# Attention with memory and two expert layers on one core: the opening in token pairs, padded queries and a new order

## The chip, the core and the metric

One Trainium2 chip, one of its cores. The engines are TensorE (PE, with its weight loads shown apart as PEld), VectorE (DVE), ScalarE (ACT), GpSimd (POOL) and SyncE (SP), which here issues most transfers. The metric is the device time of one execution in microseconds; the time of a kernel is the median of its runs.

## The reference

Attention over four sequences of 768 tokens, eight heads of 64. The sequence is cut into chunks of 32 queries; each chunk attends to 8 memory slots and to its own keys with 16 to the left and 8 to the right (64 columns in all, fewer at the sequence's ends). The result goes through two layers, 512 to 2048 to 512 each, the first with a leaky ramp, the second with a rational function of `h`.

```python
for c in range(S // 32):
    l_start, r_end = max(0, 32 * c - 16), min(S, 32 * c + 32 + 8)
    k_full = concat([mem_k, k[:, :, l_start:r_end]], axis=2)      # v_full alike
    scores = scale * q_c @ k_full.T                               # scale = 1 / sqrt(64)
    a = exp(scores - max(scores))
    out[:, :, c_start:c_end] = (a / (sum(a) + 1e-09)) @ v_full
x = out.transpose(0, 2, 1, 3).reshape(3072, 512)
h = x @ w_in;  x = maximum(0.01 * h, h) @ w_out
h = x @ w_in2
P = a0 + a1*h + a2*h*h + a3*h*h*h
y = (P / (1 + |b0|*|h| + |b1|*h*h + 1e-6)) @ w_out2
```

## The kernel before

The 3072 tokens go through the layers in six tiles of 512. Weights and activations are split into a high and a low part, so each product of the layers is three matmuls (high x high, high x low, low x high). A weight chunk is 128 of the 2048 hidden columns; there are 16 for each of the four matrices, and each is loaded once, split by `pair_scale` (ACT), `pair_join` (three whole-tile operations on DVE), `pair_hi` (a cast on ACT) and `pair_lo` (a difference). `pair_load(0, ONE_)` loads the first input chunk, `emit_first(i, ...)` runs the first layer's input matmuls of chunk i for the first tile. After the opening, the attention blocks of the later tiles are spread between the chunks' matmuls.

The order of every instruction on every engine is written out by hand (`tc.manual_schedule()`): the order of the calls is the order in each engine's queue. Every queue is in order, so an instruction that waits holds what stands behind it. SP's transfers signal through eight completion slots: an issue waits until the transfer eight issues earlier has landed.

The opening, up to the first chunks of the first layer, makes the first tile's attention: 512 tokens in U = 4 units of 128 tokens. Its functions, for unit u:

- `unit_k`, `unit_q`: four 128 x 128 transposes (`turn`, L414) of the loaded keys or queries into PSUM; keys copied by ACT into `okT` (two tiles, one for each half of the heads, early[4] and early[5]), queries scaled by ACT into `oqT`. Loads are by 128 tokens in rows of 64 floats (256 bytes) per head.
- `unit_small`: the transposed memory keys and the keys at unit borders, copied by DVE (L424, L428).
- `unit_b`: copies on GpSimd that put each key chunk also into the ring of left neighbours (L445).
- `unit_s`: scores, 32 matmuls (L464), each with one head's 32 queries as 64 x 32 weights on 64 columns; the trace has two records for each.
- `unit_m` (L472 to L476), on DVE: a mask for the first unit, the maximum, the difference. `unit_e` (L480): exp on ACT.
- `unit_n` (L486 to L489): DVE sums, adds 1e-9 (the "guard", a tiny `tensor_scalar`, L487) and takes the reciprocal (L488); then a product, on GpSimd for units 0 to 2, on DVE for unit 3.
- `unit_t` (L495 to L502): four transposes of the probabilities, copied out by ACT into `pT` (zero-padded, in two half copies, for units 0 and 1; one plain copy for 2 and 3).
- `unit_x`: values, matmuls with `vroom[u]` as weights (L514 for units 0 and 1, 16 matmuls; L527 for units 2 and 3, 32 matmuls). `vroom` holds the value rows of each window, with the 8 memory rows copied there by `room_mem` on GpSimd (four copies on 8 partitions, L418, 2048 or 1536 columns).
- `side_h`, `side_l`: attention output from PSUM into `xh` (ACT, L538) and the remainder into `xl` (DVE, L542), the first layer's input.

`heat(n)` is n matmuls of 128 columns on the identity (L966) and `warm(n)` one of n x 128 columns (L969); nobody reads their results. The last output tile is written 128 tokens at a time: 3 matmuls a chunk into one PSUM bank (L950), a copy (L955), a transfer of 256 KB (L956).

## Time and profile before

| what | value |
|---|---|
| median of 3 runs | 1138.33 us (1136.58 to 1138.68) |
| profiled execution: time, span | 1139.2 us, 1137.4 us |
| busy: PE, PEld | 1128.2 us (99%), 923.3 us (81%) |
| busy: DVE, ACT, POOL | 766.3 us (67%), 628.9 us (55%), 238.3 us (21%) |
| PE busy 0 to 32.60 us | 27.93 us |
| chain that ended last | 96% PE, 1% DVE, 1% DMA |

The profile is of one execution; its own time stands 0.9 us above the median. TensorE is busy nearly throughout, so the chain that ended last is almost all TensorE; the rest of it lies in the first 33 us. Times in the profile are counted from the span's start.

### The profile page before, as it was taken

To read this page: it belongs to the slowest core of one execution; us is meant where nothing else is said; L and a number is where in the kernel's file an instruction comes from. 1 tells how busy PE (TensorE), PEld (TensorE's weight loads), DVE (VectorE), ACT (ScalarE), POOL (GpSimd) and SP (SyncE) were. 2 spreads that over 40 slices of the span, in tenths; PEclk is the share of its full clock that TensorE was granted. 3 is DMA by queue.
4 is the path that set the end of the run, shared out by engine and by line. 5 is a ranking of instruction groups with operands and counts; after the bars stand their busy time and mean duration, and the time that the engine had idled before them with its cause. 6 is when DMAs were issued, how large, how long until landed. Compare 5 with 4: busy or idle time off the path is not lost.

```text
span 1137.4 us, 19661 instructions
## 1 busy us (share of the span) xinstructions
PE 1128.2 (99%) x7626; PEld 923.3 (81%) x7626; DVE 766.3 (67%) x1315; ACT 628.9 (55%) x1138; POOL 238.3 (21%) x274
## 2 busy tenths in 40 slices
PE   8999999999999999999999999999999999999998
PEld 6777788888888888888888888888888888888887
DVE  5988754555645555542346886887887887788775
ACT  5687522232232223223347777776776777777765
POOL 5000302132211332210000222221222222222222
PEclk9999999999999999999999999999999999999999
DMA  9967777787778778732343002001001100100001
GB/s 193 277 200 214 181 218 208 210 244 216 207 212 232 198 206 236 214 114 94 93 140 117 22 1 74 1 1 61 14 1 40 36 1 19 57 1 4 35 0 37
DMA packets 146921, 131.59 MB, mean 116 GB/s; under 512 B 61744, under 2 KB 117392, under 8 KB 146828
## 3 DMA queue, kind: packets, MB, share of 16 engines
q1 hardware_dynamic: 141604, 122.80, 37.8%
q0 software_dynamic: 4864, 7.45, 2.9%
q8 instruction: 60, 0.98, 0.4%
q14 instruction: 33, 0.27, 0.1%
q10 hardware_dynamic: 360, 0.08, 0.0%
HBM read 92.52 MB, written 37.75 MB: 115 GB/s over the span
## 4 chain that ended last, share of the span: by engine, by line
PE 96%; DVE 1%; DMA 1%; ACT 0%; issue 0%; SPq 0%; POOL 0%; DVEq 0%; POOLq 0%
PE hps L854 45%; PE acc L950 23%; PE acc L912 23%; PE psx L754 2%; PE pss L712 1%; PE pss L554 0%; DMA early<-in_q_dram 0%; PE psx L601 0%; DMA pb<-park_dram 0%; PE pss L464 0%; PE psk L377 0%; PE hps L842 0%; DMA park_dram<-pb 0%; PE psq L414 0%; PE psx L527 0%
## 5 line engine op out<-in xcount | busy, mean ns | idle before, releaser
L912 PE MATMUL acc<-g,w 128*128 128x512 f32 x1152 | 278.3, 391 | 0.0
L950 PE MATMUL acc<-w,g 128*128 128x512 f32 x1152 | 275.4, 389 | 0.0
L950 PEld LDWEIGHTS acc<-w,g 128*128 128x128 f32 x1152 | 216.3, 188 | 44.8
L912 PEld LDWEIGHTS acc<-g,w 128*128 128x128 f32 x1152 | 214.8, 188 | 45.1
L890 POOL TENSOR_TENSOR g<-R,g 128x512 fp32r<-128x512 f32 x96 | 124.7, 1299 | 503.9 <-ACT g L889 465.7
L864 ACT ACTIVATE g<-hps 128x512 fp32r<-128x512 f32 x96 | 57.4, 598 | 299.2 <-PE hps L854 299.2
L854 PE MATMUL hps<-xh,w 128*128 128x512 f32 x752 | 205.0, 395 | 0.0
L854 PE MATMUL hps<-yh,w 128*128 128x512 f32 x768 | 204.1, 389 | 0.0
L867 DVE TENSOR_TENSOR g<-s,g 128x512 fp32r<-128x512 f32 x96 | 66.2, 690 | 175.9 <-ACT s L865 172.8
L854 PEld LDWEIGHTS hps<-yh,w 128*128 128x128 f32 x768 | 144.2, 188 | 30.0
L854 PEld LDWEIGHTS hps<-xh,w 128*128 128x128 f32 x752 | 138.4, 188 | 29.5 <-DVE w L195 0.2
L677 POOL DMA_DIRECT2D vb<-in_v_dram x128 | 83.8, 656 | 260.2 <-PE psx L754 201.7
L877 ACT ACTIVATE A<-hps 128x512 f32<-128x512 f32 x96 | 57.2, 596 | 113.9 <-PE hps L854 113.9
L893 DVE SCALAR_TENSOR_TENSOR A<-A,small,pb 128x512 f32<-128x512 f32 x96 | 72.1, 751 | 56.5 <-ACT pb L878 56.4
L854 PE MATMUL hps<-yl,w 128*128 128x512 f32 x384 | 102.6, 389 | 0.0
L854 PE MATMUL hps<-xl,w 128*128 128x512 f32 x376 | 100.9, 390 | 0.0
L884 DVE SCALAR_TENSOR_TENSOR A<-A,pb 128x512 f32<-128x512 f32 x96 | 66.4, 692 | 30.2 <-ACT pb L897 30.2
L854 PEld LDWEIGHTS hps<-yl,w 128*128 128x128 f32 x384 | 72.1, 188 | 14.9
L854 PEld LDWEIGHTS hps<-xl,w 128*128 128x128 f32 x376 | 70.6, 188 | 15.4
L879 ACT ACTIVATE R<-hps,small 128x512 f32<-128x512 f32 x96 | 75.0, 782 | 0.0
L886 DVE SCALAR_TENSOR_TENSOR R<-R,small,A 128x512 f32<-128x512 f32 x96 | 72.2, 752 | 3.4
L895 DVE SCALAR_TENSOR_TENSOR R<-R,small,hps 128x512 f32<-128x512 f32 x96 | 71.8, 748 | 3.4
(126 smaller groups left out, 1140.7 us busy)
## 6 DMA issues: line engine op xcount, KB each, us to landing
wr<-in_moe_w_in_dram SPq DMA_DIRECT2D x32, 512.0 KB
wr<-in_moe_w_out_dram SPq DMA_DIRECT2D x32, 512.0 KB
park_dram<-pb SPq DMA_DIRECT2D x16, 512.0 KB
pb<-park_dram SPq DMA_DIRECT2D x64, 128.0 KB
...
```

The lines of the kernel that those rows point to most:

```text
L677: nc.gpsimd.dma_start(out=vw[r + at:r + at + n, c], in_=v[bi, hs, lo:lo + n, :].rearrange("h p d -> p h d"))
L854: nc.tensor.matmul(ps[:, :n], w_[:, ws], x_[:, kk, :], start=(kk == 0 and m == 0), stop=(kk == KC - 1 and m == 2))
L864: nc.scalar.activation(out=gh, in_=ps, func=AF.Prelu, alpha=0.01)
L867: return [lambda: nc.vector.tensor_tensor(out=gl, in0=s, in1=gh.bitcast(F32), op=ALU.subtract)]
L879: nc.scalar.activation(out=R, in_=ps, func=AF.Identity, scale=ncf[:, 3:4], bias=ncf[:, 2:3])
L884: nc.vector.scalar_tensor_tensor(out=A0, in0=A0, scalar=ONE, in1=U0, op0=ALU.add, op1=ALU.mult)
L886: nc.vector.scalar_tensor_tensor(out=R0, in0=R0, scalar=ncf[:, 0:1], in1=A0, op0=ALU.add, op1=ALU.mult)
L890: nc.gpsimd.tensor_tensor(out=gl, in0=R0, in1=gh.bitcast(F32), op=ALU.subtract)
L893: nc.vector.scalar_tensor_tensor(out=A, in0=A, scalar=babs[:, 1:2], in1=U, op0=ALU.mult, op1=ALU.add)
L895: nc.vector.scalar_tensor_tensor(out=R, in0=R, scalar=ncf[:, 1:2], in1=ps, op0=ALU.add, op1=ALU.mult)
L912: nc.tensor.matmul(acc[i][d][:, :n], w_[:, ws], g_, start=(f == 0 and m == 0), stop=(f == FC - 1 and m == 2))
L950: nc.tensor.matmul(acc[i][s], g_[:, ss], w_, start=(f == 0 and m == 0), stop=(f == FC - 1 and m == 2))
```

## The change

Six parts. (1) The first 256 tokens' keys and queries are loaded as token pairs (two consecutive tokens of one head side by side, rows of 512 bytes), in halves of the heads, and turned four pairs of columns at a time; even and odd tokens are then picked apart by copies of 64 partitions x 256 columns, on ACT for the keys and on DVE for the queries. (2) All queries stand in zero-padded form in `oqB` (early[6] and the new early[7]; both are filled with zeros first, on DVE and GpSimd), so that one matmul takes two heads: 16 matmuls a unit. (3) The warm-up is four 512-column matmuls on a zeroed tile. (4) Order: units 0 and 1 are scored together by halves of the heads, their `unit_m` follow one another, the two `room_mem` copies of the first half move behind the ring copies of unit 2, those of the second half become two transfers in SP's queue, and unit 3's product goes to GpSimd. (5) `pT` of units 2 and 3 is zero-padded too (two fills of 128 x 1024 on GpSimd, two half copies each on ACT), and their values take 16 matmuls; the last unit's second half of values is loaded in four transfers instead of two and its result lies in two banks, copied out by ACT and DVE. (6) The last 128 tokens' output matmuls, copy and transfer are done in two halves of 256 columns.

```diff
-    oqT = early[6].rearrange("p (c m) -> p c m", c=NP)
+    oqB = [t.rearrange("p (c n e m) -> p c n e m", c=NP, e=2, m=CHUNK) for t in early[6:8]]
...
+    def pairs_of(src, g, hs):
+        return src[0, hs, g * 2 * P:(g + 1) * 2 * P, :].rearrange("h (p t) d -> p h (t d)", t=2)
+
+    def load_pairs(raws, src, g, hs=slice(0, H)):
+        nc.sync.dma_start(out=raws[:, hs], in_=pairs_of(src, g, hs))
+
+    def turn_pairs(t, half, ps):
+        for i in range(H // 2):
+            nc.tensor.transpose(ps[:, i * P:(i + 1) * P], t[:, half * (H // 2) + i], ident)
+
+    def pairs_out(ps, o, to, lo, eng, op):
+        for e in range(2):
+            for t in range(2):
+                i = ps[t * 64:t * 64 + 64].rearrange("p (c e m) -> p c e m", c=HP, e=2)[:, :, e, lo:]
+                op(eng, o[e * 64:e * 64 + 64, :, to + 2 * lo + t:to + 2 * P:2], i)
...
             nc.vector.tensor_copy(out=okB[half][:, :, 0:RING, 0:NM],
-                                  in_=i[:, :, 0:NM].unsqueeze(2).to_broadcast([P, HP, RING, NM]))
...
+    def pairs_k(half, eng):
+        ps = psw.tile([P, 512], F32, tag="ps", name="psk")
+        turn_pairs(kpair, half, ps)
+        pairs_out(ps, okT[half], TAT, 0, eng, copy_on)
...
+    def pairs_q(half, eng):
+        ps = psw.tile([P, 512], F32, tag="ps", name="psq")
+        turn_pairs(qpair, half, ps)
+        for e in range(2):
+            for t in range(2):
+                i = ps[t * 64:t * 64 + 64].rearrange("p (c e n m) -> p c e n m", c=HP, e=2, m=CHUNK // 2)[:, :, e]
+                scale_on(eng, oqB[0][e * 64:e * 64 + 64, half * HP:(half + 1) * HP, :, e, t:CHUNK:2], i)
...
-        nc.scalar.mul(out=oqT[:, :, u * P:(u + 1) * P], in_=pv, mul=scale)
+        n, at = P // CHUNK, (u - 2) * P // CHUNK
+        for e, eng in enumerate(engs):
+            r = slice(e * 64, e * 64 + 64)
+            scale_on(eng, oqB[1][r, :, at:at + n, e, :], pv[r].rearrange("p c (n m) -> p c n m", m=CHUNK))
...
         for b in range(2):
...
-                        nc.tensor.matmul(ps[o:o + CHUNK, p, b, :], oqT[r, p, x:x + CHUNK],
-                                         okB[p // HP][r, p % HP, lo:hi + 1:hi - lo, :], start=True, stop=True)
-        ops[u] = ps
+            for p in range(halves[0] * HP, (halves[-1] + 1) * HP):
+                for c in range(2):
+                    n = (2 * u + b) * 2 + c
+                    lo, hi = n % RING, RING + 1 + n
+                    nc.tensor.matmul(ps[c * 64:c * 64 + 64, p, b, :],
+                                     oqB[u // 2][:, p, n % (NQ // 2)].rearrange("p e m -> p (e m)"),
+                                     okB[p // HP][:, p % HP, lo:hi + 1:hi - lo, :], start=True, stop=True)
...
-        if u >= 2:
-            return [lambda: nc.scalar.copy(out=pT[u], in_=ps)]
         return [lambda: part_of(0), lambda: part_of(1)]
...
+        if u not in oxv:
+            if u == U - 1:
+                oxv[u] = [psw.tile([P, 512], F32, tag="ps", name="psx")[:, :256] for _ in range(2)]
+            else:
+                t = (psw.tile([P, 512], F32, tag="ps", name="psx") if u >= 2 else
+                     psa.tile([P, 512], F32, tag="acc", name="psx"))
+                oxv[u] = [t[:, h * 256:(h + 1) * 256] for h in range(2)]
+                oxv[u, "all"] = t
+        xv = [t.rearrange("p (c b h m) -> p c b h m", c=HP, b=2, h=2) for t in oxv[u]]
...
+        for c in cs:
+            for p in ps:
+                for e in range(2):
+                    nc.tensor.matmul(xv[p // HP][e * 64:e * 64 + 64, p % HP, :, c, :], vroom[u][:, c, 2 * p + e, :],
+                                     pT[u][:, (2 * p + c) * 2 + e], start=True, stop=True)
...
+    def side_h(i, ps=ALL, eng=nc.scalar):
+        xv, xh, xl = side(i, ps)
+        copy_on(eng, xh, xv)
...
+            parts = (slice(0, DM // 2), slice(DM // 2, DM)) if (c, s) == (len(items) - 1, ns - 1) else (slice(0, DM),)
+            for ds in parts:
+                for m, (g_, w_) in enumerate(((gh, wh), (gh, wl), (gl, wh))):
+                    nc.tensor.matmul(acc[i][s][:, ds], g_[:, ss], w_[:, ds],
+                                     start=(f == 0 and m == 0),
+                                     stop=(f == FC - 1 and m == 2 and ds.stop == DM))
...
+                parts = (slice(0, DM // 2), slice(DM // 2, DM)) if (c, s) == (len(items) - 1, ns - 1) else (slice(0, DM),)
+                for ds in parts:
+                    nc.scalar.copy(out=e[:, ds], in_=acc[i][s][:, ds])
+                    nc.sync.dma_start(out=out[s0 + s * P:s0 + (s + 1) * P, ds], in_=e[:, ds])
...
+        cold = mall[:, 1].rearrange("p n m -> p (n m)")[:, :P]
+        nc.vector.memset(cold, 0.0)
...
-        nc.sync.dma_start(out=rows_of(kraw[0]), in_=tokens(k, 0, P))
+        nc.vector.memset(early[6], 0.0)
+        nc.gpsimd.memset(early[7], 0.0)
+        LOWER, UPPER = slice(0, H // 2), slice(H // 2, H)
+        load_pairs(kpair, k, 0, LOWER)
...
-        for t, src, u in ((qraw, q, 0), (kraw, k, 1), (qraw, q, 1), (kraw, k, 2), (qraw, q, 2), (kraw, k, 3),
-                          (qraw, q, 3)):
+        load_pairs(qpair, q, 0, LOWER)
+        load_pairs(kpair, k, 0, UPPER)
+        load_pairs(qpair, q, 0, UPPER)
+        for t, src, u in ((kraw, k, 2), (qraw, q, 2), (kraw, k, 3), (qraw, q, 3)):
             nc.sync.dma_start(out=rows_of(t[u]), in_=tokens(src, u * P, P))
...
+                hs = (slice(0, H // 2), slice(H // 2, H)) if (u, c) == (U - 1, 1) else (slice(0, H),)
+                for h in hs:
+                    for b_ in range(2):
+                        load_span(vroom[u][:, c, h], b_ * SB + NM, v, 0, u * P + b_ * QB + c * CHUNK - LCTX, W, h)
...
+                for b_ in range(2):
+                    o, i = mem_rows(1, b_)
+                    nc.sync.dma_start(out=o, in_=i)
...
-        heat(6)
-        unit_k(0, (act, act))
-        unit_q(0)
-        border = unit_small()
-        unit_b(0, pool)
+        for _ in range(4):
+            warm(4, cold)
+        pairs_k(0, act)
+        unit_b(0, pool, (0,))
+        unit_b(1, pool, (0,))
+        unit_small()
+        pairs_q(0, dve)
+        pairs_k(1, act)
+        unit_b(0, pool, (1,))
+        unit_b(1, pool, (1,))
+        unit_s(0, (0,))
+        unit_s(1, (0,))
+        pairs_q(1, dve)
+        unit_s(0, (1,))
+        unit_s(1, (1,))
+        pool.memset(pT[2], 0.0)
+        unit_k(2, (act, act))
+        unit_q(2, (act, act))
+        unit_m(0)
+        unit_m(1)
+        unit_e(0)
+        unit_b(2, pool)
+        pool.memset(pT[3], 0.0)
         room_mem(0, 0, pool)
-        room_mem(0, 1, pool)
-        heat(2)
-        unit_s(0)
-        unit_k(1, (act, act))
-        unit_b(1, pool)
-        unit_q(1)
-        unit_m(0)
-        border()
-        unit_e(0)
-        unit_k(2, (act, act))
-        unit_b(2, pool)
-        unit_q(2)
...
-        room_mem(1, 1, pool)
+        unit_b(3, pool)
+        unit_n(0, pool)
+        unit_q(3, (act, act))
         spread = unit_t(0)
         unit_s(3)
+        room_mem(0, 1, pool)
+        unit_n(1, pool)
...
+        unit_n(3, pool)
+        side_h(0)
+        pair_scale(0, ONE_)
+        run(pair_join(0, ONE_))
...
-        unit_n(3, dve)
-        run(pair_join(0, ONE_))
+        spread = unit_t(3)
+        unit_x(1)
+        unit_x(2)
+        run(spread)
...
-        unit_x(3)
+        side_l(0)
+        side_l(1)
         pair_hi(0, ONE_)
         pair_lo(0, ONE_, pool)
...
         side_h(2)
-        side_h(3)
+        unit_x(3, (0,))
+        unit_x(3, (1,), range(HP))
+        side_h(3, FORE)
+        unit_x(3, (1,), range(HP, NP))
+        side_h(3, REAR, dve)
+        side_l(2)
         emit_first(0, (0, 2))
```

The order at the places that the prediction speaks of follows. TensorE's queue at the program's start, in the kernel before: `hot` is the warm-up, `psk` and `psq` are the turned keys and queries, `pso` the memory keys and borders, `pss` the scores.

```order
L966 MATMUL hot<-ident 128x128 x6
L414 MATMUL psk<-ident,early 128x128 x4
L414 MATMUL psq<-ident,early 128x128 x4
L414 MATMUL pso<-ident,kb 128x24 x4
L966 MATMUL hot<-ident 128x128 x2
L464 MATMUL pss<-early 32x64 x32
L414 MATMUL psk<-ident,early 128x128 x4
L414 MATMUL psq<-ident,early 128x128 x4
L414 MATMUL psk<-ident,early 128x128 x4
L414 MATMUL psq<-ident,early 128x128 x4
L414 MATMUL psk<-ident,early 128x128 x4
L464 MATMUL pss<-early 32x64 x32
```

The same in the changed kernel:

```order
L994 MATMUL hot<-pm 128x512 x4
L425 MATMUL psk<-ident,early 128x128 x4
L414 MATMUL pso<-ident,kb 128x24 x4
L425 MATMUL psq<-ident,early 128x128 x4
L425 MATMUL psk<-ident,early 128x128 x4
L497 MATMUL pss<-early 64x64 x16
L425 MATMUL psq<-ident,early 128x128 x4
L497 MATMUL pss<-early 64x64 x16
L414 MATMUL psk<-ident,early 128x128 x4
L414 MATMUL psq<-ident,early 128x128 x4
L414 MATMUL psk<-ident,early 128x128 x4
L497 MATMUL pss<-early 64x64 x16
```

All four warm-up matmuls stand ahead of the first keys; the scores of the first two units stand together, in halves, behind both halves of the pairs.

DVE's queue at the program's start before, from the copies of the memory keys on (`pss` scores, `pm` probabilities, `mx` and `sm` maximum and sum):

```order
L424 COPY early<-pso 128x2x8x8 x2
L428 COPY early<-pso 128x2x8 x2
L472 MEMSET pss 32x4x16 x2
L475 TENSOR_REDUCE mx<-pss 128x8
L476 TENSOR_TENSOR pm<-pss,mx 128x512
L428 COPY early<-pso 128x2x8 x2
L486 TENSOR_REDUCE sm<-pm 128x8
L487 TENSOR_SCALAR sm<-sm 128x8
L488 RECIPROCAL sm<-sm 128x8
L475 TENSOR_REDUCE mx<-pss 128x8
L476 TENSOR_TENSOR pm_104<-pss,mx 128x512
L475 TENSOR_REDUCE mx<-pss 128x8
```

The same piece of the changed kernel:

```order
L439 COPY early<-pso 128x2x8x8 x2
L443 COPY early<-pso 128x2x2x8 x2
L455 TENSOR_SCALAR early<-psq 64x16x16 x8
L504 MEMSET pss 64x4x16
L507 TENSOR_REDUCE mx<-pss 128x8
L508 TENSOR_TENSOR pm<-pss,mx 128x512
L507 TENSOR_REDUCE mx<-pss 128x8
L508 TENSOR_TENSOR pm_104<-pss,mx 128x512
L518 TENSOR_REDUCE sm<-pm 128x8
L519 TENSOR_SCALAR sm<-sm 128x8
L520 RECIPROCAL sm<-sm 128x8
L518 TENSOR_REDUCE sm<-pm_104 128x8
```

Eight scalings of the queries now stand between the memory keys and the first mask, and both first units' maxima and differences ahead of the first sum.

GpSimd's queue in the kernel before, from the fill of `pT` of unit 0 to the two products behind the second room copies:

```order
L1001 MEMSET pb 128x1024
L1002 MEMSET pb_106 128x1024
L445 COPY early<-early 128x2x4x24 x2
L418 COPY early<-early 8x2048 x2
L445 COPY early<-early 128x2x4x24 x4
L489 TENSOR_TENSOR pm<-pm,sm 128x512
L445 COPY early<-early 128x2x4x24 x2
L418 COPY early<-early 8x1536 x2
L489 TENSOR_TENSOR pm_104<-pm_104,sm 128x512 x2
```

And in the changed kernel (the COPY of 8x2048 are the room copies, those of 128x2x4x24 the ring copies):

```order
L1007 MEMSET early 128x2048
L1037 MEMSET pb 128x1024
L1038 MEMSET pb_106 128x1024
L476 COPY early<-early 128x2x4x24 x4
L1075 MEMSET early 128x1024
L476 COPY early<-early 128x2x4x24 x2
L1082 MEMSET early 128x1024
L434 COPY early<-early 8x2048
L476 COPY early<-early 128x2x4x24 x2
L521 TENSOR_TENSOR pm<-pm,sm 128x512
L434 COPY early<-early 8x2048
L521 TENSOR_TENSOR pm_104<-pm_104,sm 128x512 x2
```

The room copies moved from ahead of nearly everything to between the ring copies and the products; three fills were added.

## Rows read from the trace of the kernel before

**Rows 1.** Busy time by stretch: bounds, length, each engine's busy us, clock, DMA share, GB/s.
```profile
32.60:116.90 84.30, 84.30 (x721) 66.76 (x721) 72.98 (x117) 63.39 (x169) 2.63 (x4) 1.00 0.77 216
116.90:1133.90 1017.00, 1015.97 (x6374) 834.68 (x6372) 673.66 (x1154) 547.88 (x938) 219.45 (x244) 1.00 0.36 104
1133.90:1137.40 3.50, 0.00 (x0) 0.00 (x0) 0.00 (x0) 0.54 (x1) 0.00 (x0) 0.99 0.62 231
```

**Rows 2.** Chain that ended last, up to 60 us: start, length, engine, tile, line.
```profile
21.73 1.05 POOL pm L489
...
22.83 0.66 PE pst L495 x4
...
26.45 0.81 issue
27.25 0.92 PE psx L527 x40
...
28.20 0.59 ACT xh L538
...
32.60 3.12 PE hps L842 x12
```

**Rows 3.** Timeline, TensorE: start, length, operation xcount [idle before and its releaser].
```profile
1.37 2.93 PE L966 MATMUL hot<-ident 128*128 128x128 f32 x12 [1.37 <-POOL ident masks.py:199]
...
4.16 1.12 PE L414 MATMUL psk<-ident,early 128*128 128x128 f32 x4
...
8.69 1.93 PE L464 MATMUL pss<-early 64*32 64x64 f32 x64
...
12.59 0.66 PE L414 MATMUL psk<-ident,early 128*128 128x128 f32 x4
...
13.17 1.10 PE L464 MATMUL pss<-early 64*32 64x64 f32 x64
...
21.03 1.02 PE L969 MATMUL hot<-ident 128*128 128x512 f32 x2
...
23.42 1.15 PE L514 MATMUL psx<-pb,early 128*64 128x64 f32 x32
```

**Rows 4.** Groups by line and shape, first 33 us: busy us, mean ns of one.
```profile
L476 DVE TENSOR_TENSOR pm<-pss,mx 128x512 f32<-128x512 f32 x4 | 2.8, 691 | 0.1
...
L499 ACT COPY pb<-pst 64x512 f32<-64x512 f32 x4 | 2.3, 580 | 0.2
...
L502 ACT COPY pmore<-pst 128x512 f32<-128x512 f32 x2 | 1.2, 588 | 0.4 <-PE pst L495 0.4
...
L1001 POOL MEMSET pb<- 128x1024 f32 x1 | 1.0, 952 | 0.0
...
L488 DVE RECIPROCAL sm<-sm 128x8 f32<-128x8 f32 x4 | 0.8, 203 | 0.1
```

**Rows 5.** Timeline, copies out of PSUM on ACT and DVE.
```profile
5.32 0.65 ACT L418 COPY early<-psk 128x256 f32<-128x256 f32 x2 [3.29 <-PE psk L414]
...
7.64 0.49 DVE L424 COPY early<-pso 128x128 f32<-128x128 f32 x2 [6.12 <-PE pso L414]
...
8.05 0.25 DVE L428 COPY early<-pso 128x16 f32<-128x16 f32 x2
```

**Rows 6.** Timeline, the room copies on GpSimd and what DVE does at the time.
```profile
6.35 3.83 POOL L418 COPY early<-early 8x2048 f32<-8x2048 f32 x2
...
10.73 0.31 DVE L472 MEMSET pss<- 32x64 f32 x2 [2.43 <-PE pss L464]
...
17.54 1.46 POOL L418 COPY early<-early 8x1536 f32<-8x1536 f32 x1
...
17.99 1.04 DVE L487 TENSOR_SCALAR sm<-sm 128x8 f32<-128x8 f32 x1
...
21.18 0.17 DVE L487 TENSOR_SCALAR sm<-sm 128x8 f32<-128x8 f32 x1
```

**Rows 7.** DMA view, first 30 us in 40 slices: GB/s of each.
```profile
GB/s 0 0 60 221 265 228 214 189 215 231 215 222 223 217 217 197 191 168 156 62 160 202 231 133 293 308 150 177 162 156 196 182 197 152 216 299 287 355 382 411
```

151 lines of the change are left out of this document (51 added, 100 removed).

## Prediction

> **What bounds the kernel now.** I read the busy time by stage first. From 32.60 us, where the second weight chunk's first matmul starts, TensorE is busy 84.30 of 84.30 us, and then 1015.97 of 1017.00 us up to 1133.9 [rows 1]. What stands behind 32.60 is therefore a fixed block of 1133.9 - 32.6 = 1101.3 us of TensorE work, and 3.5 us of output behind it. Apart from the last output tile, the diff touches only what lies ahead of 32.60. So the question is when the matmul now at 32.60 starts (call it E); a shift of E is carried whole to the end.
>
> Next I read the chain of waits backwards from E [rows 2]. E follows by 3.8 us the end of the last copy of attention output (28.20 + 0.59 = 28.79). Ahead of that copy stand the last unit's value matmuls at 27.25, after 0.81 us without any compute releaser: the last value rows had not landed. Ahead of that stand the transposes of the softmax, and GpSimd's normalising product at 21.73. So in the old opening two things end within a microsecond of one another: the softmax chain (DVE and GpSimd) and the last value load. A change has to shorten both to gain, and needs to lengthen only one to lose.
>
> **The change part by part.**
> *Warm-up.* Six 128-column matmuls on the identity took 2.93 us, 0.49 each [rows 3]. Now four 512-column ones run on a zeroed tile. That tile is DVE's first instruction, so they can start at about 1.1 instead of 1.37. [...] Four, each 0.05 shorter for running back to back, end at 5.0 if all ran at the high level and at 8.7 if all at the low one. In the old kernel the transposes at 4.16 take 1.12 and the scores at 8.69 take 1.93, against 0.66 and 1.10 at 12.59 and 13.17 [rows 3]: the rise came after 8.69. I take 7.5, nearer the low end. The old keys were transposed at 4.16, so the warm-up now stands ahead of them in TensorE's queue: the opening starts 3.3 us later. What it pays: all that follows runs at the high level. [...]
>
> *Keys as pairs.* Four transposes, 0.66: 7.5 to 8.2. ACT then makes four copies of 64 partitions x 256 columns. A copy of 64 x 512 takes 580 ns and one of 128 x 512 588 ns [rows 4]: half the partitions save nothing. So each costs as much as the old 128 x 256 copy, 0.65 / 2 = 0.33 [rows 5], and four cost 1.3: to 9.55. For two units ACT spends 8 x 0.33 = 2.6 instead of 4 x 0.33 = 1.3.
>
> *Memory keys and borders.* DVE's four copies now wait for ACT's four (they write the same tiles). Two memory copies took 0.49 and two border copies 0.25 [rows 5]: 10.3.
>
> *Queries as pairs.* They go from ACT (two 128 x 512) to DVE: eight of 64 x 256. A DVE copy of 128 columns took 0.49 / 2 = 0.245 [rows 5], an operation of 512 columns 0.69 [rows 4]; 256 columns lie between, 0.37. Four per half: 1.5, to 11.8. These 3.0 us in all are new work on DVE, the engine that makes the softmax, and now stand ahead of it.
>
> *Scores.* 64 matmul records of 32 matmuls took 1.10 at the high level, 0.034 a matmul. The padded form has 16 a unit with weights twice as wide and twice as deep, so 16 cost between 0.55 (same price each) and 1.1 (twice); I take 0.85. Lower half for both units: to 12.7. Then the upper queries' transposes 0.66 (13.4), DVE's next four 1.5 (14.9), and eight matmuls of the first unit 0.45: its scores are complete at 15.4. DVE began its softmax at 10.73 in the old kernel [rows 6]. So the softmax starts 4.7 us later.
>
> *What is given back.* Both first units come together, so DVE need not wait in between (it had idled up to 2.4 us, in the row at 10.73, and some more later). Its list from 15.4: mask 0.15, then for each of four units 2 x 0.69 for maximum and difference and 0.69 + 0.17 + 0.20 for sum, guard and reciprocal. The last product goes from DVE (0.69) to GpSimd (1.05 by the row at 21.73). The units 0 and 1 differences end at 18.3.
>
> *GpSimd's part.* Its order is now: ring copies of unit 2, a zero fill, one memory-room copy, ring copies of unit 3, product 0, the second room copy, products 1, 2, two small copies, product 3. The room copies of 8 x 2048 took 3.83 for two, 1.9 each [rows 6], at 6.35, beside nothing that mattered; now they stand in front of product 0 and product 1. Unit 2's keys are out at 17.1 (scores to 15.8, transposes 0.66, copies 0.65), so: ring 17.75, fill of 0.95 [rows 4] 18.7, room 20.6, ring 21.25. DVE's guard of unit 0 (ready at 19.0) is of the form that took 1.04 instead of 0.17 us while GpSimd was in a room copy, and ended with it [rows 6]; so it ends at 20.8, the reciprocal at 21.0. Product 0: 21.25 to 22.3. Room: 24.2. Product 1: 25.25. On DVE unit 1's sum ends at 21.7, its guard is held to 22.5, reciprocal 22.7, units 2 and 3 maximum and difference to 25.45, unit 2's sum to reciprocal 26.55. Product 2 to 27.6; unit 3's guard is held by it, reciprocal 28.0; product 3 to 29.1. Transposes 0.66: 29.8. Two half copies on ACT, 2 x 0.58 (one copy of 0.59 in the old kernel): 30.95. Last values 1.15, as the sixteen matmuls of the same form at 23.42 [rows 3]: 32.1. Their copy-out is halved over two banks and two engines, 0.35: 32.45. Then the same 3.8 as before: E = 36.25. The same adding, done on the old order, ends 0.3 too late, so 35.95: **3.4 us later than 32.60**.
>
> *The loads.* In SP's queue 29 transfers instead of 25 stand ahead of the third weights, with no more bytes from memory. The last values landed at about 27.2 [rows 2]; here they are wanted at 30.95, so this load is off the path by 3 us either way and I cost it at nothing. If that cover were gone, it would cost up to four issues. [...]
>
> *The tail.* The last tile's matmuls, copy and transfer are halved. In the 3.5 us after the last matmul the output queue still moves 231 GB/s x 3.5 us = 0.81 MB [rows 1], three of the four 256 KB transfers. The last one stands behind this stream, so a copy that ends 0.3 us sooner finds it busy; three more matmul issues cost some 0.1. I take 0 (bounds 0.2 less and 0.1 more).
>
> The profiled execution took 1139.2 us; 3.4 more are 1142.6. The median is 0.9 below the profiled time, so about 1141.7 us.
>
> **The rivals.**
> *B, DVE alone sets the pace.* If GpSimd's instructions fit into gaps and hold nothing, DVE ends its list at 18.3 + 4 x 1.06 + 4 x 0.69 = 25.3, product 3 at 26.4, transposes 27.1, copies 28.3, values 29.4, copy 29.8, E = 33.6, less 0.3: +0.7, so 1139.0. For it: DVE's lists are free of GpSimd except for the guards. Against it: the held guard at 17.99. It decides when the room copies start before 16, which the ring copies ahead of them do not allow, or when they do not hold the guard.
> *C, faster.* If the warm-up runs at the high level early (ends near 5.0, 2.5 sooner) and a 256-column operation on DVE costs what one of 128 does (1.0 sooner), the softmax starts at 11.9, and with B's list E is 29.8, if the last values have landed by 24.8. In the old opening 256-byte runs moved at 189 to 231 GB/s in most slices, the later, longer ones at 287 to 411 [rows 7]. If half of the first 2 MB, 1.05 MB, move at 300 instead of 215, that saves 4.9 - 3.5 = 1.4: they land at 25.85 instead of 27.25, half of their matmuls (0.58), the copy (0.35) and the 3.8 follow, and E is 30.6. So E is 2.0 to 2.8 us sooner; with 2.4, the time is 1135.9. Against it: every old row until 8.69 is at the low level. [...]
> *D, slower still.* If the clock rises only after the warm-up (all four at the low level, 8.7, and three sets of transposes at 1.12), the softmax starts 1.2 + 3 x 0.46 = 2.6 later: +6.0 at most, some of it taken by GpSimd's waits; about 1143.7.
> *The change doing nothing* is not among them: TensorE has no idle time in which a later opening could hide.
>
> **How the numbers follow.** A measurement of this kernel can tell about 0.2%, 2.3 us. Forecast 0.46; D 0.10; B, with what lies between it and the forecast, 0.31; C 0.13. The forecast's own lower end (less than 2.3 later) is counted with B. So slower 0.56, within 0.2% 0.31, faster 0.13. The range leaves out the far part of C and of D: 1136.4 to 1143.9. It is wide since the clock (5.0 to 8.7) and GpSimd's holds (0.7 to 3.4) are not shown by any old row in the new places.
>
> **What would show it.** In the new trace: warm-up rows ending at 6.5 to 8.7, and transposes behind them at 0.66; four ACT copies of 64 x 256 at about 0.33 each; DVE's mask near 15.4 (near 12 would mean C); a guard of about 1 us beside GpSimd's room copy; GpSimd's last product ending near 29; the second chunk's first matmul near 36 (33.5: B; 30: C); TensorE dense behind it. The forecast is wrong if that matmul comes before 35, or if TensorE later shows idle time that the old one hasn't.

## The result and the profile after

The changed kernel takes 1146.48 us (median of 7 runs, 1145.45 to 1147.12) against 1138.68 for the kernel before, measured beside it (7 runs, 1136.58 to 1143.14): 7.8 us slower by the medians; the ratio of the means is 1.0063, 95% interval 1.0044 to 1.0081. Forecast was slower by 3.4 us, 1141.7, with a range to 1143.9. The direction was right and the size less than half; the time lies above the range.

Call E, as the prediction does, the start of the second weight chunk's first matmul. By stretch, the profile after (bounds, length, each engine's busy us, granted clock, DMA share, GB/s):

```profile
0.00:40.46 40.46, 28.80 (x333) 20.64 (x333) 24.96 (x54) 19.80 (x39) 18.07 (x28) 0.92 1.04 249
40.46:1141.48 1101.02, 1099.85 (x7095) 901.67 (x7095) 747.32 (x1270) 610.65 (x1105) 221.44 (x248) 1.00 0.39 110
1141.48:1145.30 3.82, 0.00 (x1) 0.00 (x0) 0.00 (x0) 0.65 (x2) 0.00 (x0) 1.00 0.61 218
```

In the chain of waits E is this row:

```profile
40.46 3.10 PE hps L866 x12
```

E moved from 32.60 [rows 2] to 40.46, by 7.86 us. From E to the end of the last matmul there are 1101.0 us, against 1101.3 [rows 1], and 3.8 behind it against 3.5. So all of the loss is made in the opening and carried whole to the end, as the prediction has it; the question is only what is in those 7.86.

TensorE's opening in the timeline after (start, length, operation, xcount, idle time before it and its releaser), which answers to [rows 3]:

```profile
1.06 5.75 PE L994 MATMUL hot<-pm 128*128 128x512 f32 x8 [1.06 <-DVE early L1004]
...
6.65 0.60 PE L425 MATMUL psk<-ident,early 128*128 128x128 f32 x4
...
7.53 0.66 PE L425 MATMUL psq<-ident,early 128*128 128x128 f32 x4
...
11.36 1.43 PE L497 MATMUL pss<-early 128*64 128x64 f32 x32 [2.74 <-DVE early L455]
...
12.72 1.12 PE L425 MATMUL psq<-ident,early 128*128 128x128 f32 x4
...
15.75 1.97 PE L497 MATMUL pss<-early 128*64 128x64 f32 x32 [1.91 <-DVE early L455]
...
17.66 1.12 PE L414 MATMUL psk<-ident,early 128*128 128x128 f32 x4
...
33.21 1.15 PE L550 MATMUL psx<-pb,early 128*64 128x64 f32 x32
...
34.20 2.04 PE L550 MATMUL psx<-early 128*64 128x64 f32 x64
```

The warm-up ends, and the keys' transposes start, at 6.65. The transposes of the lower queries then run at the high level (0.66 at 7.53), TensorE waits 2.74 us for DVE's query scalings, and what follows is slow again: 1.12 for the upper queries' four transposes, 1.97 for the upper scores, 1.12 for unit 2's keys. The granted clock says the same (same view as the first):

```profile
12.50:15.00 2.50, 1.34 (x10) 0.82 (x6) 1.10 (x3) 0.00 (x0) 0.11 (x1) 0.50 1.14 186
...
17.50:20.00 2.50, 2.29 (x17) 1.89 (x14) 2.27 (x4) 1.14 (x3) 0.66 (x3) 0.72 1.06 201
```

It is at 0.50, the low level, from 12.5 to 17.5, and back between 17.5 and 20 (0.72 on the mean). In the old opening the level was low up to 8.69, rose once and stayed [rows 3]. That is read from durations: in both profiles the granted clock stands at 1.00 throughout the first 10 us, beside rows that took longer than later ones of their form (here 5.75 for the four warm-up matmuls, and 1.02 for one like them at 27.89; before, 1.12 and 0.66 for the keys' transposes), so for the program's start it does not tell the level.

The three other engines around the softmax, from the timeline after; this answers to [rows 6]:

```profile
16.95 0.11 DVE L504 MEMSET pss<- 64x64 f32 x1 [1.35 <-PE pss L497]
...
18.86 0.62 ACT L434 COPY early<-psk 128x240 f32<-128x240 f32 x2 [7.84 <-PE psk L414]
...
19.42 1.19 ACT L453 ACTIVATE early<-psq 64x512 f32<-64x512 f32 x2
...
20.64 0.63 ACT L512 ACTIVATE pm<-pm 128x512 f32<-128x512 f32 x1
...
20.81 1.88 POOL L434 COPY early<-early 8x2048 f32<-8x2048 f32 x1
...
21.30 0.69 DVE L518 TENSOR_REDUCE sm<-pm 128x8 f32<-128x512 f32 x1 [1.46 <-ACT pm L512]
...
22.02 0.70 DVE L519 TENSOR_SCALAR sm<-sm 128x8 f32<-128x8 f32 x1
...
23.24 1.03 POOL L521 TENSOR_TENSOR pm<-pm,sm 128x512 f32<-128x512 f32 x1
...
28.14 1.17 ACT L531 COPY pb<-pst 64x512 f32<-64x512 f32 x2 [1.25 <-PE pst L527]
...
29.34 0.63 ACT L512 ACTIVATE pm<-pm 128x512 f32<-128x512 f32 x1
29.70 0.35 POOL L1105 COPY kT<-early 128x32 f32<-128x32 f32 x2
...
30.08 0.69 DVE L518 TENSOR_REDUCE sm<-pm 128x8 f32<-128x512 f32 x1 [1.51 <-POOL kT L1105]
```

The mask starts at 16.95 (10.73 before). Unit 0's exponential (L512) runs at 20.64, although its input is there at 18.5: ACT's queue has unit 2's key and query copies (18.86 and 19.42) ahead of it. So DVE stands idle for 1.46 us before the sum (L518) at 21.30. Product 0 starts at 23.24. The guard (L519) at 22.02 takes 0.70 beside the room copy at 20.81, and 0.17 at 28.16, where GpSimd stands idle. Unit 3's exponential at 29.34 stands behind the two copies of `pT` of unit 1 (28.14), and DVE is idle again, for 1.5 us, until 30.08. The profile puts that down to GpSimd's small copy, which ends at 30.05, only 0.08 after the exponential; experiment e2 below tells them apart.

The new narrow copies in the groups by shape (busy us, mean ns of one), beside [rows 4, 5]:

```profile
L455 DVE TENSOR_SCALAR early<-psq 64x256 f32<-64x256 f32 x8 | 3.4, 421 | 2.7 <-PE psq L425 2.7
L434 ACT COPY early<-psk 64x256 f32<-64x256 f32 x8 | 3.1, 382 | 5.9 <-PE psk L425 5.3 <-DVE early L443 0.6
```

In these two profiles the loss has two parts. The mask came 6.2 us later (16.95 against 10.73), and from the mask to E it took 23.5 us instead of 21.9, 1.6 more. The forecast had 4.7 for the first and a gain of 1.0 for the second (15.4 to 36.25 is 20.85). The split is that of two single executions: in e8 below, the same old opening had its mask at 8.62 and E at 31.88, which would make it 8.3 and 0.3.

### The profile page after: what moved, and what is told of

Read it like the earlier page. It is cut to its first block, busy times and chain, and to the rows that moved or that the text cites. A ratio compares the mean times of both kernels' runs of the same rounds, so it can differ in the third digit from the quotient of the medians.

```text
span 1145.3 us, 19306 instructions
## 1 busy us (share of the span) xinstructions
PE 1128.7 (99%) x7427; PEld 922.3 (81%) x7427; DVE 772.3 (67%) x1323; ACT 631.1 (55%) x1145; POOL 239.5 (21%) x276
## 4 chain that ended last, share of the span: by engine, by line
PE 95%; DVE 1%; SPq 1%; DMA 1%; ACT 1%; issue 0%; POOL 0%; ACTq 0%; DVEq 0%; POOLq 0%
PE hps L878 45%; PE acc L976 23%; PE acc L936 22%; PE psx L778 2%; PE pss L736 1%; SPq L319 1%; PE hot L994 1%; PE pss L578 0%; DMA pb<-park_dram 0%; PE psx L625 0%; POOL pm L521 0%; PE psk L376 0%; DMA park_dram<-pb 0%; PE hps L866 0%; PE psx L550 0%
## 5 line engine op out<-in xcount | busy, mean ns | idle before, releaser
L878 PEld LDWEIGHTS hps<-xh,w 128*128 128x128 f32 x752 | 138.4, 188 | 29.1 <-DVE w L194 0.2
```

Of the source, the lines that this page charges most:

```text
L878: nc.tensor.matmul(ps[:, :n], w_[:, ws], x_[:, kk, :], start=(kk == 0 and m == 0), stop=(kk == KC - 1 and m == 2))
```

## The experiments

All change the changed kernel, unless it is said otherwise, and compute the whole of it. The table has the three numbers that the argument needs: the start of the first mask on DVE, E, and the time (median of 4 to 12 runs where it says timed, else one execution). The median of the kernel before was 1138.3 beside e9 to e12 (16 runs, 1137.03 to 1140.95) and 1139.1 beside e13 and e14 (23 runs, 1137.37 to 1144.93).

| kernel | mask | E | time |
|---|---|---|---|
| before | 10.73 | 32.60 | 1138.7, timed |
| changed | 16.95 | 40.46 | 1146.5, timed |
| e1 room copies early | 16.98 | 38.75 | 1144.4 |
| e2 exponential 3 first | 16.61 | 38.54 | 1144.4 |
| e3 / e11 clock kept | 16.72 / 15.80 | 39.36 / 38.52 | 1145.0 / 1144.0, timed |
| e4 no token pairs | 13.83 | 37.26 | 1143.3 |
| e5 exponential 0 first | 16.96 | 41.33 | 1147.8 |
| e6 no pairs, order mended | 13.35 | 34.25 | 1141.4 |
| e7 / e10 two warm-ups | 13.41 / 15.62 | 36.06 / 39.12 | 1141.4 / 1143.1, timed |
| e8 old kernel, tail in halves | 8.62 | 31.88 | 1138.3 |
| e9 rebuilt | 9.23 | 32.35 | 1138.5, timed |
| e12 old kernel, new warm-up | 11.03 | 38.54 | 1142.0, timed |
| e13 rebuilt, fewer transfers | 9.56 | 32.47 | 1139.2, timed |
| e14 pairs kept, order mended | 15.33 | 36.36 | 1143.6, timed |

An E of one execution is good to about 0.7 us at best, and a mask to about 2: e8 has the old opening unchanged, and its E is 31.88 instead of 32.60, its mask 8.62 instead of 10.73. Where a row has two runs, they are two executions of one kernel.

**e1, room copies early.**

```diff
+        room_mem(0, 0, pool)
+        room_mem(0, 1, pool)
         pool.memset(pT[2], 0.0)
...
         pool.memset(pT[3], 0.0)
-        room_mem(0, 0, pool)
...
-        room_mem(0, 1, pool)
         unit_n(1, pool)
```

> The changed kernel with its two room copies on GpSimd moved ahead of the first zero fill of pT, into the stretch where GpSimd stands idle (12.6 to 19.3 us in the changed kernel's trace); nothing else. E is the start of the second chunk's first matmul, 40.46 us in the changed kernel. Theory 1 (several queues hold one another: room copies in GpSimd's queue, exponentials behind copies in ACT's queue, the clock's fall): product 1 no longer waits for a room copy and ends about 1.9 us sooner, and E comes 2.0 us sooner, 38.5. Theory 2 (DVE's new query scalings alone set the time): the room copies hold nothing that matters, E stays within 0.3 of 40.5.

Product 1 starts at 24.26 instead of 26.30 (it was to end 1.9 sooner), and E is 38.75, 1.7 us sooner, with the mask where it was (16.98):

```profile
24.26 1.04 POOL L521 TENSOR_TENSOR pm<-pm,sm 128x512 f32<-128x512 f32 x1 [0.41 <-DVE sm L520]
```

Theory 1 holds here: the room copies in front of the products cost 1.7 us at E.

**e2, the exponential of unit 3 first.**

```diff
         unit_x(0)
-        run(spread)
         unit_e(3)
+        run(spread)
```

> The changed kernel with the exponential of unit 3 put ahead of the two copies of pT of unit 1 in ACT's queue; nothing else. Theory 1: the exponential runs at 27.5 instead of 29.3, DVE's 1.5 us of idle time ahead of unit 3's sum falls to nothing, product 3 ends about 1.3 us sooner, and of that 0.9 reaches E (39.6), since the copies and value matmuls of units 1 and 2 then stand in front of unit 3's. Theory 2: DVE's work is in the way, E within 0.3 of 40.5.

```profile
25.41 1.04 POOL L521 TENSOR_TENSOR pm<-pm,sm 128x512 f32<-128x512 f32 x1
...
27.59 0.65 DVE L518 TENSOR_REDUCE sm<-pm 128x8 f32<-128x512 f32 x1
...
29.27 1.04 POOL L521 TENSOR_TENSOR pm<-pm,sm 128x512 f32<-128x512 f32 x1
```

Unit 3's sum now follows without a gap (27.59), so it was the exponential that DVE had waited for, not GpSimd's small copy. From product 1's start to product 3's start it was 31.36 - 26.30 = 5.06 us, and now 29.27 - 25.41 = 3.86: 1.2 us less, as theory 1 expected (1.3). E came 1.9 sooner, more than the 0.9 expected; 0.9 of that is there before product 1 already (25.41 against 26.30), where the edit changes nothing. In this execution the upper queries' transposes and scores ran at the high level (0.66 at 13.27, 1.15 at 15.84). So about 1.0 is the edit's own.

**e3 and e11, the clock kept.**

```diff
+        for _ in range(3):
+            warm(4)
         unit_s(0, (0,))
         unit_s(1, (0,))
         pairs_q(1, dve)
+        for _ in range(2):
+            warm(4)
```

> The changed kernel with three 512-column warm-up matmuls on the identity behind the pairs' first three sets of transposes (TensorE stood idle there from 8.63 to 11.36) and two more behind the upper queries' transposes; nothing else. Theory 1: the granted clock stays at the high level, the upper queries' transposes take 0.66 instead of 1.12, the upper scores about 1.1 instead of 1.97, the mask starts 1.1 to 1.3 us sooner (15.7), and E comes about 1.2 sooner, 39.2. Theory 3 (the clock falls anyway, or what it costs is hidden behind DVE): E within 0.3 of 40.5.

> The kernel of e3 once more, timed (one look gave E = 39.36 and 1145.0 us, with a rise 1.5 us later than in the changed kernel's profile). Theory 1: with the clock kept the median is 1.5 to 2.5 us below the changed kernel's 1146.5. Theory 3: within 1 us of it.

```profile
12.46 0.66 PE L425 MATMUL psq<-ident,early 128*128 128x128 f32 x4
...
15.03 1.15 PE L497 MATMUL pss<-early 128*64 128x64 f32 x32 [0.20 <-DVE early L455]
15.80 0.11 DVE L504 MEMSET pss<- 64x64 f32 x1 [0.91 <-PE pss L497]
...
21.23 1.03 POOL L521 TENSOR_TENSOR pm<-pm,sm 128x512 f32<-128x512 f32 x1
```

The rows are those of the second execution, e11. It started as the changed kernel's did (keys at 6.65), so the two profiles can be laid side by side: with the level kept, the upper scores take 1.15 instead of 1.97, the mask starts 1.15 us sooner (15.80), product 0 starts 2.0 sooner (21.23 instead of 23.24), and E comes 1.94 sooner. Timed, it is 1144.04 against 1146.48, 2.4 us less, or 2.1 less when each is taken against the kernel before beside it. Theory 3 falls: the clock's second fall costs about 2 us.

**e4, no token pairs.** Units 0 and 1 are loaded, turned and copied as units 2 and 3 are.

```diff
-        load_pairs(kpair, k, 0, LOWER)
+        nc.sync.dma_start(out=rows_of(kraw[0]), in_=tokens(k, 0, P))
...
-        pairs_k(0, act)
...
+        unit_k(0, (act, act))
+        unit_b(0, pool)
+        unit_small()
+        unit_q(0, (dve, dve))
+        unit_k(1, (act, act))
+        unit_b(1, pool)
+        unit_s(0)
+        unit_q(1, (dve, dve))
+        unit_s(1)
```

> The changed kernel without the token pairs: units 0 and 1 are loaded by 128 tokens, turned and copied as units 2 and 3 are, scores are made unit by unit; queries still go zero-padded into the new tiles, on DVE, in two copies of 64 x 512 a unit; all other parts of the change stay. Theory 2 (the pair form's many narrow copies and its wait for two units cost the time): the first mask starts near 13.4 instead of 16.95, and E comes 3 us sooner, 37.4. Theory 1: the mask starts as early, but the exponential of unit 0 still stands behind unit 2's copies on ACT and the room copies still hold GpSimd, so that at most half of it, 1.5 us, reaches E: 39.

The mask starts at 13.83, 3.1 us sooner, and E is 37.26, 3.2 us sooner. Theory 2 has this one: what the mask gains reaches E whole, and theory 1's claim that half of it would be swallowed by the other holds was wrong. Holds that follow one another in one chain all move together. Not all of the 3.1 is the pairs' own work: in this execution the level did not fall (0.66 at 11.67, 1.15 at 13.90; e11 puts that at 1.15 at the mask), while the keys' transposes started 0.8 later than in the changed kernel (7.47), which leaves some 2.8 for the pair form with its scores by halves.

**e5, the exponential of unit 0 first.**

```diff
-        unit_k(2, (act, act))
-        unit_q(2, (act, act))
         unit_m(0)
         unit_m(1)
         unit_e(0)
+        unit_k(2, (act, act))
+        unit_q(2, (act, act))
```

> The changed kernel with the exponential of unit 0 put ahead of the key and query copies of unit 2 in ACT's queue; nothing else (E was 40.46). Theory 1a (GpSimd's order holds product 0): the exponential runs at 18.5 instead of 20.6 and DVE's idle time of 1.46 us ahead of unit 0's sum goes, but unit 2's copies, the ring copies behind them and the room copy come 0.4 us later, so product 0 starts as late as before and E moves by -0.3 to +0.4. Theory 1b (the late exponential is what holds product 0): E comes 1.0 to 1.4 us sooner, near 39.2.

```profile
18.56 0.63 ACT L512 ACTIVATE pm<-pm 128x512 f32<-128x512 f32 x1 [7.65 <-DVE pm L508]
...
19.76 0.68 DVE L518 TENSOR_REDUCE sm<-pm 128x8 f32<-128x512 f32 x1
...
23.59 1.03 POOL L521 TENSOR_TENSOR pm<-pm,sm 128x512 f32<-128x512 f32 x1
...
25.26 1.83 PE L497 MATMUL pss<-early 128*64 128x64 f32 x32
```

The exponential runs at 18.56 and DVE's idle time goes, but product 0 starts at 23.59, not sooner than 23.24: GpSimd reaches it only behind the ring copies, and these now come later. So 1a holds up to product 0, and 1b falls: the late exponential of unit 0 did not hold product 0. That E is 0.9 later lies outside 1a's band too; unit 3's scores took 1.83 here instead of 1.15 (the row at 25.26), the low level once more.

**e6, no pairs and the order mended.** The edits of e1, e2, e4 and e5, and unit 1's value matmuls ahead of unit 3's transposes:

```diff
-        spread = unit_t(3)
         unit_x(1)
+        spread = unit_t(3)
         unit_x(2)
```

> The kernel of e4 (no token pairs, E = 37.26) with all order edits together: room copies early as in e1, exponentials 3 and 0 first as in e2 and e5, and unit 1's value matmuls ahead of unit 3's transposes. Theory 1 (the holds add up): 37.26 less 1.7 (e1) less 1.0 (the part of e2 that stands behind product 1) less 0.5 is E = 34.0, and it cannot fall below 32.1, DVE's own list from the mask at 13.8. Theory 4 (the holds hide one another, or the last value load binds): E stays above 35.5.

E is 34.25 against 34.0 expected: the holds add up, and theory 4 falls for this kernel. What unit 1's value matmuls gain by their new place is in this sum and has no run of its own.

**e7 and e10, two warm-ups.**

```diff
-        for _ in range(4):
+        for _ in range(2):
             warm(4, cold)
```

> The changed kernel with two 512-column warm-up matmuls instead of four; nothing else. Theory 5 (the warm-up's length stands on the path): the first transposes start at about 4.6 instead of 6.7 and take 1.12 instead of 0.66, the scores are made some 1.5 us sooner, and E comes 1.0 to 1.5 us sooner, 39.2. Theory 6 (the warm-up pays for itself): the clock stays at the low level through the first scores and the unit 2 transposes, which costs 0.46 for each of four sets of transposes and 0.8 for each half of the scores, and E is 40.5 to 42.

> The kernel of e7 once more, timed (one look gave E = 36.06 and 1141.4 us; the granted clock was high from 4.3 us on and never fell). Theory 5 (the shorter warm-up is what gained): the time is 3.5 to 5.5 us below the changed kernel's 1146.5, in every round. Theory 6b (the clock's early rise in that one execution is what gained, and it varies): the rounds spread over 2 us or more and their median is 1 to 3 us below the changed kernel.

The first keys' transposes in the two executions of this one kernel, and the upper queries' (e7, then e10):

```profile
4.28 0.60 PE L425 MATMUL psk<-ident,early 128*128 128x128 f32 x4
...
10.07 0.66 PE L425 MATMUL psq<-ident,early 128*128 128x128 f32 x4
```

```profile
4.63 1.06 PE L425 MATMUL psk<-ident,early 128*128 128x128 f32 x4
...
11.38 1.12 PE L425 MATMUL psq<-ident,early 128*128 128x128 f32 x4
```

In e7 the level was high at 4.28 and stayed, in e10 it was low at 4.63 and fell again before 11.38. E is 36.06 in the one and 39.12 in the other. Timed, the kernel takes 1143.12 (1142.18 to 1144.90), 3.4 us less than the changed kernel. So no expectation has it alone: the shorter warm-up is worth about 3 us, since it starts the chain 2 to 2.4 us sooner in either execution, and the moment at which the clock rises and falls makes up to 3 us between executions of one kernel. In the changed kernel's profile the two extra matmuls bought a level that the opening then lost again.

**e8, the tail alone**, on the kernel before (part 6 of the change and nothing else; the diff is the one under the change).

> The kernel before with only the last output tile's matmuls, copy and transfer in two halves. The stretch from the last matmul's end to the end of the span is 3.5 us in the kernel before. Theory 1: 3.3 to 3.8, since the last transfer waits for the three ahead of it. Rival: the earlier half transfer shortens it by 0.5 or more, 3.0 or less. E stays at 32.6.

From the last matmul's end to the end it is 4.08 us, beside 3.5 in the kernel before and 3.8 in the changed one:

```profile
1132.42:1136.50 4.08, 0.00 (x1) 0.00 (x0) 0.00 (x0) 0.65 (x2) 0.00 (x0) 0.90 0.57 205
```

That is no gain, and 0.3 more than expected; the rival falls.

The opening is the old one, and its second execution went another way than [rows 3] and [rows 6] show: the queries' first transposes at 5.81 took 0.68 already, the mask starts at 8.62 instead of 10.73, and E is only 0.7 sooner. The timeline and the chain of waits:

```profile
8.62 0.31 DVE L472 MEMSET pss<- 32x64 f32 x2 [1.09 <-PE pss L464]
```

```profile
23.09 5.48 DMA wr<-in_moe_w_in_dram
...
31.88 3.11 PE hps L842 x12
```

In this chain the softmax does not stand. The second chunk's weights land at 28.57, and E stands behind their split on ACT and DVE. So 2.1 us taken from the softmax brought 0.7.

**e12, the old kernel with the new warm-up.**

```diff
-        heat(6)
+        for _ in range(4):
+            warm(4)
         unit_k(0, (act, act))
```

> The kernel before with only its first six 128-column warm-up matmuls replaced by four of 512 columns on the identity. Theory 5: the first transposes start at 6.9 to 7.7 instead of 4.16; all behind them then runs at the high level, which gives back some 0.5 for each set of transposes and 0.8 for the first scores, so the mask starts at about 11.7 to 12.5 instead of 10.73, and E comes 1.0 to 1.8 us later, 33.6 to 34.4. Theory 6: the high level gives all of it back, E within 0.4 of 32.6.

The keys were turned at 7.86, 3.7 us later than before, but the mask started only 0.3 later (11.03), as all behind the warm-up ran at the high level (0.60 for the keys' transposes, 1.10 for the first scores at 9.82): theory 6 on this point, measured against the profile of the kernel before (against e8, with the same opening, the mask is 2.4 later). E was 38.54 all the same. TensorE stopped in the middle of a group of like matmuls:

```profile
22.82 0.33 PE L495 MATMUL pst<-ident,pm 128*128 128x128 f32 x1 [1.17 <-issue]
...
26.13 1.46 PE L527 MATMUL psx<-pmore,early 64*64 64x32 f32 x82
...
27.06 0.44 SPq L325 DMA_DIRECT2D qr<-in_q_dram  x1
...
30.81 1.61 PE L527 MATMUL psx<-pmore,early 64*64 64x32 f32 x46 [3.21 <-issue]
...
33.22 4.19 PE L842 MATMUL hps<-xh,w 128*128 128x512 f32 x8
```

It was not waiting for the value rows. The last of them were issued by 22.97 (23.04 before), and the issue at 27.06 is the eighth behind, so they had landed by then: an issue waits for the transfer eight issues earlier, ACT's issues counted in (in the profile of the kernel before, SP's fourth issue, the ninth with ACT's five, stood 1.2 us, to 4.13, for the landing of the first). The profile names nothing that this wait of 3.21 us is for ("issue"). What it goes with is the number of instructions: it comes behind TensorE's 470th matmul record, and so does the wait of 0.81 us at 27.25 in the kernel before [rows 2], though behind the other warm-up that is another matmul, the 78th record of its group instead of the 82nd. The waits of 1.17 at 22.82 and of 0.47 at 16.80 lie 125 and 252 records ahead of it. Whether TensorE's instructions themselves came late was not shown; up to 36 us the DMA view counts four transfers of an instruction queue, as in the kernel before. The matmuls behind the wait ran at the low level (4.19 for the eight at 33.22, which took 2.21 in the kernel before). This profile is of the slowest of five runs (1137.30 to 1143.62; the ratio is 1.0025, 1.0009 to 1.0042), and the kernel before spread as widely; what the warm-up alone is worth in the old kernel is open.

**e9 and e13, a rebuilt opening.** e9 is e6 with two warm-ups, the first units' queries scaled on ACT, and the zero fills of `pT` behind product 1. e13 also takes four transfers out of SP's queue.

```diff
-        unit_q(0, (dve, dve))
+        unit_q(0, (act, act))
...
+        unit_n(1, pool)
+        pool.memset(pT[2], 0.0)
+        pool.memset(pT[3], 0.0)
```

> The kernel of e6 (no token pairs, all order edits, E = 34.25) with two warm-up matmuls instead of four, the queries of units 0 and 1 scaled on ACT (two copies of 64 x 512 each) instead of DVE, and the two zero fills of pT of units 2 and 3 moved behind product 1 on GpSimd. Theory 1: the mask starts near 10.5 instead of 13.35, product 0 near 15 instead of 18.2, and E is 30.5 to 32, so that the time is 0.1 to 0.2% below the kernel before. Theory 4 (another resource binds now: the last value rows, the first weights): product 0 comes early, but E stays at 33 or above, and the time is that of the kernel before or up to 0.2% above it.

The chain of waits of e9:

```profile
23.21 4.33 DMA early<-in_v_dram
...
27.68 0.47 PE psx L550 x8
```

The mask starts at 9.23, 1.5 us ahead of the old kernel's profile (0.6 behind e8's), unit 3's values wait 0.56 us for the landing of their last rows at 27.55, and E is 32.35. The time is that of the kernel before: ratio 1.0004, interval 0.9995 to 1.0013. Theory 4 holds in the time and in the wait for rows; E lies between the two bands (up to 32, and from 33).

The edit of e13 on top of e9 (the one above is e9's on top of e6):

```diff
             if u == 2:
                 pair_load(0, ONE_)
-                for b_ in range(2):
-                    o, i = mem_rows(1, b_)
-                    nc.sync.dma_start(out=o, in_=i)
...
-                hs = (slice(0, H // 2), slice(H // 2, H)) if (u, c) == (U - 1, 1) else (slice(0, H),)
+                hs = (slice(0, H),)
...
+        room_mem(0, 0, pool)
         unit_k(1, (act, act))
         unit_b(1, pool)
...
-        room_mem(0, 0, pool)
         room_mem(0, 1, pool)
+        room_mem(1, 0, pool)
...
+        room_mem(1, 1, pool)
         pool.memset(pT[2], 0.0)
```

> The kernel of e9 with four transfers fewer in SP's queue: the memory rows of the second half are copied on GpSimd in its idle time instead of by two transfers, and the last unit's values are loaded in two transfers for the second half instead of four. In e9 the last values landed at 27.55 and unit 3's last value matmuls waited 0.56 us for them. Theory 4 (the loads, held by SP's issues, bind once the softmax is early): the last issue of values ends 1.5 to 2 us sooner than 23.2, the values land near 26, and E comes 0.5 to 1.2 us sooner, 31.2 to 31.8; the time is 0.05 to 0.15% below the kernel before. Theory 7 (what binds is the DMA engines' work, which is the same): the values land within 0.5 of 27.5, E stays at 32 or above, and the time is that of the kernel before within 0.1%.

```profile
22.26 1.05 POOL pm L521
...
26.39 0.58 ACT early L531
```

The last issue of values ends at 21.67 instead of 23.63, 2.0 us sooner (1.5 to 2 expected), and the value matmuls no longer wait for rows; E is 32.47 and the time ratio 0.9995 (0.9981 to 1.0009). Neither theory has it whole: the rows came sooner, but the chain of waits above runs through a GpSimd product at 22.26 and the last copy of `pT` at 26.39: with GpSimd's extra copies the softmax took over where the load had been. No version was measured faster than the kernel before.

**e14, the pairs kept and the order mended.** The changed kernel with two warm-ups and the edits of e1, e2, e5, e6's value order and the moved fills.

```diff
-        for _ in range(4):
+        for _ in range(2):
             warm(4, cold)
...
+        room_mem(0, 0, pool)
+        room_mem(0, 1, pool)
...
         unit_n(1, pool)
+        pool.memset(pT[2], 0.0)
+        pool.memset(pT[3], 0.0)
```

> The changed kernel with its token pairs kept and all else mended: two warm-up matmuls, room copies early, exponentials 0 and 3 first, zero fills behind product 1, unit 1's values ahead of unit 3's transposes; queries of the pairs still scaled on DVE. Theory 2 (the pair form costs 3 us wherever the rest stands): the mask starts at 13.4 to 14.5, about 4 to 5 us later than e9's 9.2, E is 35 to 36, and the time 0.25 to 0.35% above the kernel before. Theory 1 (with the holds gone the rest of the pairs' cost hides behind the loads): E is 33 or less.

The mask starts at 15.33 and E is 36.36; timed 1143.57, ratio 1.0034 (1.0021 to 1.0047). Theory 2 holds in the time and in kind; the mask came 0.8 and E 0.4 later than its bands. Mending order and warm-up takes E from 40.46 to 36.36, 4.1 us, and what is left to e9, 4.0 us, is the pair form with its scalings on DVE. The clock fell once more in this execution (the upper scores took 1.98), so between 1 and 2 us of the 4.0 are the level and not the pairs' work (e11: 1.15 at the mask, 1.94 at E). From the mask to E it is now 21.0 us instead of 23.5.

## Why the prediction was wrong

*Where the time is decided.* Right: E moved 7.86 us and the time 7.8. The reading of the old opening behind it was wrong in one row: the 0.81 us ahead of 27.25 were taken for value rows that had not landed, and by e12 that wait goes with the count of TensorE's instructions. That loads end together with the softmax is right, but e8 shows it, by a wait of 0.29 us for value rows and by the weights at 28.57.

*The warm-up.* It was to end at 7.5 (5.0 to 8.7). It ended at 6.65 in the changed kernel and at 7.5 in e2, e3 and e4. Right in size. The two bounds take 1.9 us for a 512-column matmul at the low level, the author's estimate from the 128-column ones, which no row of the old kernel shows, and 1.0 at the high one. In e10 two took 3.78, 1.9 each, with the level still low behind them (1.06 at 4.63), and in the changed kernel one took 1.02 (27.89). Wrong is the sentence behind it, "all that follows runs at the high level": that a level once up stays was the author's assumption, and the runs went both ways: it stayed in e4, e6, e7, e9 and e13, and fell in the changed kernel. This is the step that failed first, and the largest: the forecast's 0.66 for the upper queries' transposes was 1.12, its 0.85 and 0.45 for scores were 1.43 and about 1.2, and unit 2's keys were late with them. The working itself makes the gap: TensorE has nothing to do while DVE scales (2.74 us), and then a level that has been paid for is lost. The trace shows the fall behind a wait for DVE (0.50 from 12.5 us on, behind the idle time from 8.63 to 11.36); with that wait filled, the same transposes took 0.66 (e11, 12.46). Rival D had put the danger into a late rise, 1143.7; it was a second fall, and e11 prices it at about 2 us: 1.15 at the mask, 2.0 at product 0, 1.94 at E.

*The narrow copies.* ACT's cost 0.38 each instead of 0.33, DVE's 0.42 instead of 0.37 (groups above). The step that half the partitions save nothing was right (on ACT 382 ns for 64 x 256 and 375 for 128 x 256, both in the changed kernel); the price by interpolation was 15% low, 0.7 us along the chain up to the mask. The eight on DVE were forecast at 3.0 us and took 3.4.

*The scores.* Sixteen padded matmuls took 1.15 at the high level (e11, 15.03), not 0.85: just above the sum's upper bound of 1.1, and as much as the 32 narrow ones of the old kernel (1.10, [rows 3]). Half the number of score matmuls saved TensorE nothing.

*The softmax's start.* 15.4 forecast, 16.95 measured: 1.55 late, of which e11 shows 1.15 to be the clock's. Product 0 was 1.99 late, and that is the clock's whole: with the level kept it starts at 21.23 (e11), forecast 21.25. So the other misses cancel, which is luck: the warm-up ended 0.85 sooner than forecast, the narrow copies cost 0.7 more, the scores about 0.6 more, and GpSimd's copies and fill ahead of product 0 came out shorter (3.9 us, from 19.34 to 23.27, instead of 4.15).

*GpSimd's room copies and the held guard.* Right in kind: the guard took 0.70 and 0.76 beside GpSimd's instructions instead of 0.17, and the copies' move is worth 1.7 at E (e1).

*ACT's queue.* This step is missing, and it is the largest error of method. The prediction walked DVE's and GpSimd's queues instruction by instruction, and took ACT's exponentials to run when their input was there. Two of them stood behind copies that wait for TensorE. The first cost nothing that e5 could find, as product 0 waited for GpSimd's copies all the same. The second did: product 3 ended at 32.57 instead of 29.1, 1.5 us more than product 0's delay, and e2 shows that hold to be worth 1.2 at product 3. It could be seen in the forecast's own times: product 1 ends at 25.25, its transposes at 25.9, the two copies at 27.1 and the exponential behind them at 27.7, and the forecast lets unit 3's sum begin at 26.55.

*The values.* Unit 3's 1.15 us were set behind its own copies. In TensorE's queue the matmuls of units 1 and 2 stand in front of them: 96 records in all (33.21 and 34.20), and they end at 36.24, 4.1 late, 0.7 more than product 3. This is read from the rows; only e6 moves these matmuls, together with all else.

Added up: 2.0 for the clock, 1.5 on the way to product 3 (1.2 of it ACT's queue) and 0.7 for the values are 4.2 us, which is the way from the worked E of 36.25 to 40.46. The forecast had then taken 0.3 off, by what the same adding missed in the old order, and that was missing too.

*The loads.* "Off the path" is right for the changed kernel, where the value matmuls wait for no transfer. But rival C, faster, could hardly have come out as priced: e9, without the pairs, had a softmax earlier than C asks (9.23 instead of 11.9), and E was 32.35, with 0.56 us of it a wait for value rows. What the 512-byte runs gave can be read against e4, which has the rest of the change: SP issued the first weights at 13.80 instead of 14.68 there (15.85 in the old kernel), so about 0.9 us. The last issue of values, behind four more transfers, ended at 22.29, 0.8 us sooner than in the old kernel.

*The tail.* Nothing gained, as forecast; 3.8 and 4.1 us instead of 3.5, which is 0.2 and 0.5 above the bound of 0.1 more.

*The size.* The forecast let each operation on ACT and TensorE run when its input was there; in in-order queues an operation can only be later than that, never sooner, so the sum was a lower bound on this point. The range went 2.2 us above the forecast and 5.3 below it; on this evidence it should have been the other way round.
